# First stage of u and last step of a kernel block in 64-row tiles, in the slot behind PV

## The chip, the core and the metric

One core of a Trainium2 chip (trn2). The metric is the device time of one execution in microseconds; three timed runs of the kernel before are at hand, and one profiled execution. Engines: PE multiplies matrices, ACT, DVE and POOL do element-wise work, SP issues the DMAs. PSUM is the memory that PE writes; the kernel holds it as eight tiles of 128 rows by 512 columns.

## What is computed

Two independent parts, whose results stand side by side in the output. Part A is a long convolution of `u` with a kernel `K` that is first made from complex exponentials; part B is softmax attention with 16 heads of 28. L = S = 2048 and D = 448, all in float32.

```
K  = 2 * Re(einsum("dn,dnl->dl", C, exp(A*dt * pos)))       # 448 kernels of 2048
ya = irfft(rfft(u^T, 2L) * rfft(K, 2L))[:L]^T + u * D_skip
q, k, v = heads(x @ wqkv);  yb = softmax(q k^T * scale) v @ wo
out = concat([ya, yb], -1)
```

## The kernel before

Attention sets the frame. After a setup of some 250 us (projections, seeds of K, first maxima) a loop of 256 steps runs: 4 groups of 4 heads, 4 query chunks of 512, 16 key tiles of 128. Inside a step the order is written out by hand and kept on every engine:

```
ORDER = ('m0','s0','m1','s1','v','f','pv','f','v','k','m2','s2','m3','s3','v')
```

`m0` to `m3` are matmuls for row maxima of a later query chunk (tile `pm`, 128*128, emptied by ACT as `rl` for m0 and by DVE for the rest). `s0` to `s3` are score matmuls (tile `pss`), each followed by an exponential on ACT (`p`). `pv` adds up probabilities times values of the step before: four matmuls of 128 rows by 32 columns side by side into `po`. A matmul on plain float32 appears in the trace as two instructions, so pv counts as x8. The two `f` are slots: each takes at most one job of other work (`slot`). The first stands ahead of PV, the second behind it. `v` hands DVE one operation of a block's powers, `k` starts blocks and hands POOL theirs.

What the slots do, in the order of preference: urgent pieces of attention (sums, scale, end of maxima), output projections (`p_due`), pieces of kernel blocks (`m_due`), pieces of u (`u_due`), and, from step 192 on, the products of the spectra (`f_slot`).

- A *kernel block* `b` (56 of them, one begun every 3.5 steps) makes eight of the 448 kernels: two products of `e` and `g` (part0, `k_mm`), whose results ACT copies to `ko`, and a last step (part1): `ko` times the cosines and sines of `w1`, the first stage of its Fourier transform, copied by ACT to `yk` and stored. Their due steps are 4, 5 and 6 after the block's begin.
- *u*, the transform of the input, has a first stage of 16 jobs (`u_stage1`) and a second of 16 (`u_stage2`). A job of the first loads rows of u (tile `ua`), multiplies by the cosine half of `w1` in one slot and by the sine half in another, copies both by ACT to `ub`, and stores to `yu_d`. The second reads `yu_d` with the constants `m2u`.

`w1` is block diagonal: four blocks of 32 by 32 in 128 rows by 128 columns, one half for cosines and one for sines. `mm32` cuts a product into column tiles of 32. Of the four column tiles that a row of the array meets, three hold zeros for it.

The jobs and the maxima take their PSUM tiles from one ring of three (`w_tile`): `pm0`, `pm1`, `pm2` in turn. A matmul into a tile waits until the tile's last user has been emptied.

Of the kernel before, what the change touches and what calls it, by code (L numbers as in the profile page):

```python
# [18 lines left out]
D = 448  # L19
# [71 lines left out]
def body(ctx, tc, a, out):  # L91
# [25 lines left out]
    nc.sync.dma_start(ident, a["ident"])  # L117
    sel = const.tile([128, HG], F32, name="sel")
    kones = const.tile([128, 1], F32, name="kones")
    w1 = const.tile([128, 2, 128], F32, name="w1")  # L120

    att, k0_st = ExitStack(), ExitStack()
    ps_w, n_ring = [None, 3], [0]
# [12 lines left out]
    def mm32(o, w, x_, start, stop, at=0):  # L136

        for i in range(w.shape[-1] // 32):
            c = slice(32 * i, 32 * i + 32)
            nc.tensor.matmul(o[c], w[:, c], x_, start=start, stop=stop, tile_position=(0, at + 32 * i))  # L140


    kt_g, kd_g, q_u, m_u, mh_u, o_u, rl_u = {}, {}, {}, {}, {}, {}, {}

# [67 lines left out]
    with ExitStack() as st:  # L212
# [54 lines left out]
        half_pi = s_p.tile([128, 1], F32, name="half_pi")  # L267
        nc.gpsimd.memset(half_pi, TWO_PI / 4)
        nc.sync.dma_start(sel, a["sel"])
        nc.sync.dma_start(w1, a["w1"])  # L270
        for k in range(NCK):
            for s in (1, 0):
                src = wns[k][:, s, :].rearrange("p (g h e) -> p g h e", g=G, e=DH)
# [293 lines left out]
    def u_stage1(q):  # L567
        t_ = {}

        def load():  # L570
            u_in = t_["in"] = kq_p.tile([128, 8, CI], F32, name="ua", bufs=2)[:, :4]
            for j in range(4):
                nc.sync.dma_start(u_in[32 * j:32 * j + 32], bass.AP(
                    tensor=u_a.tensor, offset=u_a.offset + 4 * q * D + j * CI, ap=[[N2 * D, 32], [D, 4], [1, CI]]))

        def part(c):
            if c == 0:
                t_["out"] = kq_p.tile([128, 2, 4, CI], F32, name="ub", bufs=2)
            u_in, yt = t_["in"], t_["out"]
            pw = w_tile()  # L580
            mm32(pw[:, :D], w1[:, c, :], u_in.rearrange("p n i -> p (n i)"), start=True, stop=True)
            nc.scalar.activation(yt[:, c].rearrange("p n i -> p (n i)"), pw[:, :D], AF.Copy)
            if c == 1:
                for j in range(4):
                    nc.sync.dma_start(yu_d[8 * q:8 * q + 8, :, j * CI:(j + 1) * CI].rearrange("r k i -> k r i"),
                                      yt[32 * j:32 * j + 32].rearrange("p c n i -> p (c n) i"))
        return [load, lambda: part(0), lambda: part(1)]

    def u_stage2(m):
        t_ = {}  # L590
# [84 lines left out]
    def k_mm(b):  # L675
        t_ = {}

        def part0(i):
            pw = w_tile()
            e, g = egs[b] if i == 0 else egs.pop(b)  # L680
            for n, (h, c) in enumerate(((0, 0), (0, 1), (1, 0), (1, 1))):
                for j in range(4):
                    x_ = h * 8 + i * 4 + j
                    nc.tensor.matmul(pw[32 * j:32 * j + 32, :N2], g[:, c, x_, :], e[:, c, x_, :],
                                     start=n == 0, stop=n == 3, tile_position=(0, 32 * j))
            if i == 0:
                t_["ko"] = g_p.tile([128, 2, N2], F32, name="ko", bufs=2)
            nc.scalar.activation(t_["ko"][:, i], pw[:, :N2], AF.Copy)

        def part1():  # L690
            ko = t_["ko"]
            pw = w_tile()
            for i in range(2):
                for c in range(2):
                    mm32(pw[64 * c:64 * c + 64, i * 128:(i + 1) * 128], ko[:, i, :], w1[:, c, :], True, True, 64 * c)
            yk = g_p.tile([128, N1, 4, 2], F32, name="yk", bufs=2)
            nc.scalar.activation(yk.rearrange("p k j i -> p i j k"),
                                 pw[:, :256].rearrange("p (i j k) -> p i j k", i=2, j=4), AF.Copy)
            nc.sync.dma_start(yk_d[b // NBF][:, :, b % NBF], yk.rearrange("p (m k) j i -> p m (k j i)", k=4))
        return [lambda: part0(0), lambda: part0(1), part1]  # L700

# [178 lines left out]
            u_jobs[i][0]()  # L880

    def u_part(i, c):
        u_jobs[i][1 + c]()
        if c and i not in (14, 15):
            u_load(i + 2)
        if c and i == 15:
            u_load(16)
            u_load(17)
        if c and i == 31:
            load_wo()  # L890

    u_load(0)
    u_load(1)
    u_due = collections.deque((3 + UP * i + (UP / 2) * c + (4 if i > 15 else 0), i, c) for i in range(32) for c in range(2))
    k_due = collections.deque(range(NB))
    m_due = collections.deque()

# [56 lines left out]
        urgent.clear()  # L954
        urgent.extend(q)

    def slot(s_):
        n_slot[0] += 1
        if urgent and urgent[0][0] <= n_slot[0]:
            urgent.popleft()[2]()  # L960
        elif s_ >= NS and f_slot(s_, "s"):
            pass
        elif p_due and p_due[0][0] <= s_:
            p_due.popleft()[1]()
        elif m_due and m_due[0][0] <= s_:
            m_due.popleft()[1]()
        elif u_due and u_due[0][0] <= s_:
            u_part(*u_due.popleft()[1:])
        else:
            f_slot(s_, "s") or f_slot(s_, "f")  # L970
# [6 lines left out]
    def k_begin(s_):  # L977
        if not (k_due and K0 + k_due[0] * KP <= s_ and k_due[0] in egs and not powers["e"] and not powers["g"]):
            return
        b = k_due.popleft()  # L980
        k_start(b)
        powers["g"] += g_powers(b)
        powers["e"] += [lambda i=i, q=q: e_power(b, i, q) for i in range(3) for q in range(3)]
        p0, p1, p2 = k_mm(b)

        def m1():
            p1()
            done["mm"] = b
        m_due.extend((s_ + KD + i, t_) for i, t_ in enumerate((p0, m1, p2)))
        last[0] = b  # L990

    last = [None]
# [13 lines left out]
    for s in range(NS):  # L1006
        u, kt = divmod(s, NK)
        sm = s + NK + LEAD
        if s == 12 * NK:
            k0_st.close()  # L1010
            f_p["s", 0] = f_p["s", 1] = pool(f0_st, "f0_p", side="right")
            f_ready["s", 0], f_ready["s", 1] = s, NS
        if s >= 12 * NK and f_ready["s", 1] == NS and not (k_due or m_due or powers["g"] or powers["e"]):
            g_st.close()
            ps_st.close()
            ps_w[:] = pool(ps_st, "ps_f", 4, PSUM), 1
            f_ready["s", 1] = s + F1
        if kt == 12 and u // NQ == G - 1:
            load_og(u)
        late[0] = s + NK + LEAD > NS  # L1020
        if u % NQ == NQ - 1 and u < NU - 1 and kt % 4 == 2:
            load_v(u // NQ + 1, kt // 4)
        if sm < NS and sm // NK % NQ == NQ - 1 and sm % NK % 4 == 0 and sm % NK and sm // (NQ * NK) + 1 < G:
            load_kd(sm // (NQ * NK) + 1, sm % NK // 4 - 1)
        if sm < NS and sm % (NQ * NK) == 0 and sm:
            load_kd(sm // (NQ * NK), HG - 1)
        if kt % 4 == 1 and u % NQ == 1 and u // NQ + 1 < G:
            load_k(u // NQ + 1, kt // 4, k_pools[(u // NQ + 1) % 2])
        if kt == 2:
            if u + 2 < NU:  # L1030
                load_q(u + 2)
        ps = []
        for op in ORDER:
            if op[0] == "s":
                ps.append(s_mm(u, kt, int(op[1])))
            elif op[0] == "f":
                slot(s)
            elif op[0] == "v":
                vec()
            elif op == "k":  # L1040
                k_next()
                k_begin(s)
                k_seed(s)
                for _ in range(3):
                    if powers["e"]:
                        powers["e"].popleft()()
            elif op == "pv":
                if prev:
                    pv_step(*prev)
                    if prev[1] == NK - 1:  # L1050
                        fin(prev[0], s)
            elif sm < NS:
                max_mm(sm // NK, sm % NK, int(op[1]))
        for _ in range(FX if late[0] else 0):
            slot(s)
        if sm < NS and sm % NK == NK - 1:
            def end(un=sm // NK):
                max_end(un, w_tile())
                max_put(un)
            max_join(sm // NK)  # L1060
            soon_slot(UG[0], end)
        k_next()
        prev = (u, kt, ps)
# [11 lines left out]
def constants():  # L1075
# [9 lines left out]
    n1, k1 = np.arange(N1), np.arange(N1)  # L1085
    n2, k2 = np.arange(N2), np.arange(N2)
    th = 2 * np.pi * np.outer(n1, k1 + 0.25) / N1
    w1 = np.zeros((2, 128, 128))
    wb = np.zeros((2, 2, N1, 2, N1))
    for j in range(4):  # L1090
        w1[0, 32 * j:32 * j + 32, 32 * j:32 * j + 32] = np.cos(th)
        w1[1, 32 * j:32 * j + 32, 32 * j:32 * j + 32] = np.sin(th)
    for h in range(2):
        wb[h, 0, :, h, :] = np.cos(th).T / L
        wb[h, 1, :, h, :] = np.sin(th).T / L
    k["w1"] = w1.transpose(1, 0, 2)
    k["wb"] = wb.transpose(0, 1, 2, 4, 3).reshape(128, N2)
    ph = 2 * np.pi * ((k1[:, None, None] + 0.25) * n2[None, :, None] / L + n2[None, :, None] * k2[None, None, :] / N2)
    c, s = np.cos(ph).transpose(1, 0, 2), np.sin(ph).transpose(1, 0, 2)
    m2 = np.zeros((2, N2, N1, 2, 64))  # L1100
    m2[0, :, :, 0], m2[0, :, :, 1] = c, s
    m2[1, :, :, 0], m2[1, :, :, 1] = -s, c
    k["m2u"] = m2.reshape(2, 16, 4, N1, 128).transpose(1, 0, 2, 3, 4).reshape(128, N1, 128)
    wa = np.zeros((2, 64, N1, N2, 2))
    ct, st = c.transpose(2, 1, 0), s.transpose(2, 1, 0)
    wa[0, ..., 0], wa[0, ..., 1] = ct, -st
# [23 lines left out]
```

## Time and profile before

| | |
|---|---|
| timed runs | 1301.66, 1305.03, 1306.4 us; median 1305.03 |
| profiled execution | 1301.1 us from the first to the last instruction (its span; the page has no other time for it) |
| PE busy | 1228.2 us, 94% of the span |
| ACT, DVE, POOL busy | 952.4, 948.0, 871.1 us |
| u, first stage on PE | 256 instructions of 448 columns |
| last steps of blocks on PE | 896 instructions of 128 columns |
| ACT copies | `ub` 128x448 x32, mean 550 ns; `yk` 128x256 x56, mean 703 ns |

A row of the order of time reads: start, length, engine, line, operation, out<-in, rows*columns of the tile, shape, count; in brackets what the engine waited for. Matmuls run into each other, so a row's length holds the end of the pipe too, and the distance of starts tells what a matmul costs. `w` is `w1` (numbers are left out of names). All rows of the loop have line 75, the helper that records them; names tell them apart.

### The profile page before, as it was taken

The numbers are of one execution on the slowest core, as the hardware profiler recorded it, in microseconds if no ns is written. First come the engines' busy times: TensorE is split into PE (matmuls) and PEld (weight loads), VectorE is DVE, ScalarE is ACT, GpSimd is POOL, SyncE is SP. The second block draws the span as 40 slices with busy tenths as digits, with TensorE's granted clock in tenths as the row PEclk, the third lists the DMA queues.
The fourth block names the chain that finished last, engine by engine and source line by source line (L and its number), as shares of the span: only waits on it lengthen the run. The fifth ranks groups of instructions, "written<-read, shape, count | busy, mean of one in ns | idle before, by whom it ended". The sixth has DMA issues, their size and how long they took to land.

```text
span 1301.1 us, 33177 instructions
## 1 busy us (share of the span) xinstructions
PE 1228.2 (94%) x12625; PEld 701.0 (54%) x12625; DVE 948.0 (73%) x2106; ACT 952.4 (73%) x2068; POOL 871.1 (67%) x736
## 2 busy tenths in 40 slices
PE   6878985899999999999999999999999999999997
PEld 5657763355555555555555555555555555544433
DVE  5887896987777887787788888888888655645111
ACT  4775763488888888888888888888887766756552
POOL 3676683298888878888869999998996212424421
PEclk9888997999999999999999999999999999999999
DMA  6677769835866555458644131733425453647656
GB/s 194 203 258 244 249 206 294 237 77 124 195 137 149 124 146 148 140 147 231 181 126 96 54 95 32 182 91 83 103 51 148 153 158 133 201 144 244 198 162 174
DMA packets 200088, 205.35 MB, mean 158 GB/s; under 512 B 95993, under 2 KB 158521, under 8 KB 197881
## 3 DMA queue, kind: packets, MB, share of 16 engines
q1 hardware_dynamic: 199928, 203.23, 56.2%
q8 instruction: 100, 1.64, 0.5%
q14 instruction: 60, 0.48, 0.1%
HBM read 120.73 MB, written 82.18 MB: 156 GB/s over the span
## 4 chain that ended last, share of the span: by engine, by line
PE 71%; DVE 10%; DMA 6%; POOL 5%; ACT 3%; issue 3%; SPq 0%; POOLq 0%; ACTq 0%; DVEq 0%
PE pm L75 40%; PE pss L75 16%; PE po L75 15%; DVE tri L75 2%; DVE mx L75 2%; POOL e L75 1%; POOL qhat L75 1%; DMA k<-hl 1%; ACT tri L75 1%; DVE qhat L75 1%; DVE sg L75 1%; DMA tri<-in_B_wqkv 1%; DVE px L75 1%; DMA khat<-k 1%; DMA ut<-in_A_u 1%
## 5 line engine op out<-in xcount | busy, mean ns | idle before, releaser
L75 ACT ACTIVATE p<-pss 128x512 f32<-128x512 f32 x1024 | 560.9, 609 | 111.6 <-PE pss L75 108.6
L75 PE MATMUL pss<-qhat,khat 128*128 128x512 f32 x1024 | 402.5, 399 | 1.5 <-ACT p L75 1.4
L75 DVE TENSOR_REDUCE mx<-pm 128x1 f32<-128x512 f32 x500 | 321.4, 684 | 109.2 <-PE pm L75 107.1
L75 PE MATMUL pm<-khat,qhat 128*128 128x512 f32 x749 | 326.3, 438 | 3.4 <-DVE mx L75 2.1
L75 POOL TENSOR_TENSOR e<-e,sdb 128x256 f32<-128x256 f32 x168 | 202.0, 1202 | 116.2 <-ACT e L75 61.2
L75 PE MATMUL po<-p,v 128*32 128x512 f32 x2048 | 269.1, 594 | 0.0
L75 POOL TENSOR_TENSOR e<-e,eu 128x256 f32<-128x256 f32 x168 | 248.4, 1478 | 13.2
L75 PEld LDWEIGHTS pm<-khat,qhat 128*128 128x128 f32 x749 | 141.0, 189 | 199.7 <-ACT p L75 47.8
L75 DVE CUSTOM_DVE_ANT_0 rl<-pm,rl 128x512 f32<-128x512 f32 x249 | 171.4, 688 | 65.2 <-ACT rl L75 61.5
L75 PEld LDWEIGHTS pss<-qhat,khat 128*128 128x128 f32 x1024 | 190.2, 188 | 45.7 <-issue 10.8
L75 POOL TENSOR_TENSOR eu<-e,sdb 128x256 f32<-128x256 f32 x168 | 202.2, 1203 | 0.0
L75 POOL TENSOR_TENSOR p<-pr,pr 64x448 f32<-64x448 f32 x64 | 73.3, 1145 | 158.5 <-PE pm L75 133.2
L75 ACT ACTIVATE rl<-pm 128x512 f32<-128x512 f32 x249 | 150.8, 606 | 20.4 <-PE pm L75 20.4
L75 DVE TENSOR_TENSOR g<-g,zg 128x128 f32<-128x128 f32 x392 | 162.1, 413 | 3.4
L75 PE MATMUL pm<-xh,khat 112*128 112x512 f32 x256 | 94.1, 451 | 23.2 <-DVE hl L75 11.1
L75 PE MATMUL pm<-kdif,qhat 128*128 128x512 f32 x249 | 100.5, 404 | 2.6 <-DMA v<-v 1.3
L75 DVE TENSOR_TENSOR zg<-g,zg 128x128 f32<-128x128 f32 x224 | 88.0, 393 | 5.0
L75 PEld LDWEIGHTS pm<-e,g 128*32 128x32 f32 x3584 | 57.2, 109 | 43.8 <-issue 16.1
L75 DVE TENSOR_TENSOR pr<-pm,ub 128x448 f32<-128x448 f32 x64 | 37.0, 619 | 56.4 <-PE pm L75 42.0
L75 PEld LDWEIGHTS pm<-xh,khat 112*128 112x128 f32 x256 | 54.2, 217 | 39.4 <-DVE hl L75 12.9
L75 PE MATMUL pm<-e,g 128*32 128x64 f32 x3584 | 73.0, 222 | 1.9 <-POOL e L75 1.9
L75 ACT ACTIVATE y<-pm 128x448 f32<-128x448 f32 x48 | 26.5, 553 | 58.2 <-PE pm L75 33.8
(134 smaller groups left out, 1470.3 us busy)
## 6 DMA issues: line engine op xcount, KB each, us to landing
sdb<-sd SPq DMA_DIRECT2D x56, 336.0 KB
khat<-k SPq DMA_DIRECT2D x64, 256.0 KB
qhat<-q SPq DMA_DIRECT2D x64, 256.0 KB
sd<-sg SPq DMA_DIRECT2D x8, 1456.0 KB
k<-hl SPq DMA_DIRECT2D x16, 512.0 KB
q<-hl SPq DMA_DIRECT2D x16, 512.0 KB
mw<-in_mw SPq DMA_DIRECT2D x16, 512.0 KB
sd<-qhat SPq DMA_DIRECT2D x8, 896.0 KB
```

Of the source, the lines that this page charges most:

```text
L75: i = f(*args, **kw)
```

## The change

`w1` becomes `w2`, of the same size, without the zeros. Each product has a contraction of 64 rows instead of 128, and there are two of them for the two halves of the rows, at row positions 0 and 64, each into a PSUM tile of its own.

- First stage of u: one job (`both`) instead of two halves. It takes two tiles of the ring, issues eight matmuls of 64 rows by 32 columns and 448 columns of u, and two ACT copies of 128x448. Whole rows of u are loaded, in two DMAs instead of four; the store is one DMA instead of four. The order of rows in `yu_d` changes, and the constant `m2u` with it.
- Last step of a block: sixteen matmuls of 64 rows by 32 columns and 64 columns of `w2` instead of eight of 128 rows and 128 columns; two tiles of the ring; two ACT copies of 128x128 instead of one of 128x256.
- `slot` learns whether it stands behind PV. Ahead of PV the two-tile jobs (a block's last step, u's first stage) are passed over, and the next kind in the order of preference may go.

```diff
+        def both():
+            pw = [w_tile() for _ in range(2)]
+            for i in range(4):
+                c = slice(32 * i, 32 * i + 32)
+                for h in range(2):
+                    nc.tensor.matmul(pw[h][c, :D], w2[half[h], 0, c], t_["in"][half[h]], start=True, stop=True,
+                                     tile_position=(64 * h, 32 * i))
+            yt = kq_p.tile([128, 2, D], F32, name="ub", bufs=2)
+            for h in range(2):
+                nc.scalar.activation(yt[:, h], pw[h][:, :D], AF.Copy)
+            nc.sync.dma_start(yu_d.rearrange("(q h r) k d -> q (r k) h d", q=16, h=2)[q], yt)
...
         def part1():
             ko = t_["ko"]
-            pw = w_tile()
+            pw = [w_tile() for _ in range(2)]
             for i in range(2):
                 for c in range(2):
-                    mm32(pw[64 * c:64 * c + 64, i * 128:(i + 1) * 128], ko[:, i, :], w1[:, c, :], True, True, 64 * c)
+                    for j in range(2):
+                        for r in range(2):
+                            n = 64 * c + 32 * j
+                            nc.tensor.matmul(pw[r][n:n + 32, 64 * i:64 * i + 64], ko[half[r], i, 32 * j:32 * j + 32],
+                                             w2[half[r], 1, 64 * c:64 * c + 64], start=True, stop=True, tile_position=(64 * r, n))
...
-            nc.scalar.activation(yk.rearrange("p k j i -> p i j k"),
-                                 pw[:, :256].rearrange("p (i j k) -> p i j k", i=2, j=4), AF.Copy)
+            for r in range(2):
+                nc.scalar.activation(yk[:, :, 2 * r:2 * r + 2].rearrange("p k j i -> p i j k"),
+                                     pw[r][:, :128].rearrange("p (i j k) -> p i j k", i=2, j=2), AF.Copy)
...
-    u_due = collections.deque((3 + UP * i + (UP / 2) * c + (4 if i > 15 else 0), i, c) for i in range(32) for c in range(2))
+    u_due = collections.deque((3 + UP * i + (UP / 2) * c + (4 if i > 15 else 0), i, c) for i in range(32) for c in range(2) if i > 15 or c)
...
-    def slot(s_):
+    def slot(s_, second=True):
...
-        elif m_due and m_due[0][0] <= s_:
+        elif m_due and m_due[0][0] <= s_ and (second or not m_due[0][2]):
             m_due.popleft()[1]()
-        elif u_due and u_due[0][0] <= s_:
+        elif u_due and u_due[0][0] <= s_ and (second or u_due[0][1] > 15):
...
-                slot(s)
+                slot(s, "pv" in ORDER[:n])
```

More of the change, by code (lines that the diff above doesn't have):

```diff
@@ L119, in body @@
     kones = const.tile([128, 1], F32, name="kones")
-    w1 = const.tile([128, 2, 128], F32, name="w1")
+    w2 = const.tile([128, 2, 128], F32, name="w2")
     att, k0_st = ExitStack(), ExitStack()
@@ L140, in mm32 @@
             nc.tensor.matmul(o[c], w[:, c], x_, start=start, stop=stop, tile_position=(0, at + 32 * i))
+    half = [slice(0, 64), slice(64, 128)]
     kt_g, kd_g, q_u, m_u, mh_u, o_u, rl_u = {}, {}, {}, {}, {}, {}, {}
@@ L269, in body @@
         nc.sync.dma_start(sel, a["sel"])
-        nc.sync.dma_start(w1, a["w1"])
+        nc.sync.dma_start(w2, a["w2"])
         for k in range(NCK):
@@ L570, in load @@
         def load():
[L571 to L579, printed above, removed]
-            pw = w_tile()
[L581 to L587, printed above, removed]
+            u_in = t_["in"] = kq_p.tile([128, 8, CI], F32, name="ua", bufs=2).rearrange("p n i -> p (n i)")[:, :D]
+            for h in range(2):
+                nc.sync.dma_start(u_in[half[h]], u_a.rearrange("(p q h) d -> q h p d", q=16, h=2)[q, h])
+        def both():
[6 more added lines that the diff above has]
+            yt = kq_p.tile([128, 2, D], F32, name="ub", bufs=2)
+            for h in range(2):
+                nc.scalar.activation(yt[:, h], pw[h][:, :D], AF.Copy)
+            nc.sync.dma_start(yu_d.rearrange("(q h r) k d -> q (r k) h d", q=16, h=2)[q], yt)
+        return [load, both]
     def u_stage2(m):
@@ L691, in part1 @@
             ko = t_["ko"]
-            pw = w_tile()
+            pw = [w_tile() for _ in range(2)]
             for i in range(2):
                 for c in range(2):
-                    mm32(pw[64 * c:64 * c + 64, i * 128:(i + 1) * 128], ko[:, i, :], w1[:, c, :], True, True, 64 * c)
+                    for j in range(2):
[3 more added lines that the diff above has]
+                                             w2[half[r], 1, 64 * c:64 * c + 64], start=True, stop=True, tile_position=(64 * r, n))
             yk = g_p.tile([128, N1, 4, 2], F32, name="yk", bufs=2)
-            nc.scalar.activation(yk.rearrange("p k j i -> p i j k"),
-                                 pw[:, :256].rearrange("p (i j k) -> p i j k", i=2, j=4), AF.Copy)
+            for r in range(2):
+                nc.scalar.activation(yk[:, :, 2 * r:2 * r + 2].rearrange("p k j i -> p i j k"),
+                                     pw[r][:, :128].rearrange("p (i j k) -> p i j k", i=2, j=2), AF.Copy)
             nc.sync.dma_start(yk_d[b // NBF][:, :, b % NBF], yk.rearrange("p (m k) j i -> p m (k j i)", k=4))
@@ L882, in u_part @@
     def u_part(i, c):
-        u_jobs[i][1 + c]()
+        u_jobs[i][1 + c if i > 15 else 1]()
         if c and i not in (14, 15):
@@ L988, in m1 @@
             done["mm"] = b
-        m_due.extend((s_ + KD + i, t_) for i, t_ in enumerate((p0, m1, p2)))
+        m_due.extend((s_ + KD + i, t_, i == 2) for i, t_ in enumerate((p0, m1, p2)))
         last[0] = b
@@ L1032, in body @@
         ps = []
-        for op in ORDER:
+        for n, op in enumerate(ORDER):
             if op[0] == "s":
@@ L1087, in constants @@
     th = 2 * np.pi * np.outer(n1, k1 + 0.25) / N1
-    w1 = np.zeros((2, 128, 128))
+    w2 = np.zeros((2, 2, 64, 2, 64))
     wb = np.zeros((2, 2, N1, 2, N1))
-    for j in range(4):
-        w1[0, 32 * j:32 * j + 32, 32 * j:32 * j + 32] = np.cos(th)
-        w1[1, 32 * j:32 * j + 32, 32 * j:32 * j + 32] = np.sin(th)
+    for c, t in enumerate((np.cos(th), np.sin(th))):
+        for j in range(2):
+            w2[0, :, j::2, c, 32 * j:32 * j + 32] = t
+            w2[1, :, 32 * j:32 * j + 32, c, 32 * j:32 * j + 32] = t
     for h in range(2):
@@ L1095, in constants @@
         wb[h, 1, :, h, :] = np.sin(th).T / L
-    k["w1"] = w1.transpose(1, 0, 2)
+    k["w2"] = w2.reshape(2, 128, 128).transpose(1, 0, 2)
     k["wb"] = wb.transpose(0, 1, 2, 4, 3).reshape(128, N2)
@@ L1102, in constants @@
     m2[1, :, :, 0], m2[1, :, :, 1] = -s, c
-    k["m2u"] = m2.reshape(2, 16, 4, N1, 128).transpose(1, 0, 2, 3, 4).reshape(128, N1, 128)
+    k["m2u"] = m2.reshape(2, 2, 16, 2, N1, 128).transpose(2, 3, 0, 1, 4, 5).reshape(128, N1, 128)
     wa = np.zeros((2, 64, N1, N2, 2))
```

## The prediction

> **What bounds the kernel now.** I read the page first, then busy time by stretches, then the order of time on PE and ACT inside single steps.
>
> ```profile
> span 1301.1 us, 33177 instructions
> PE 1228.2 (94%) x12625; PEld 701.0 (54%) x12625; DVE 948.0 (73%) x2106; ACT 952.4 (73%) x2068; POOL 871.1 (67%) x736
> PE   6878985899999999999999999999999999999997
> PE 71%; DVE 10%; DMA 6%; POOL 5%; ACT 3%; issue 3%; SPq 0%; POOLq 0%; ACTq 0%; DVEq 0%
> 290.00:460.00 170.00, 169.42 (x2045) 92.85 (x2044) 132.84 (x316) 141.30 (x317) 138.31 (x108) 1.00 0.63 143
> 700.00:900.00 200.00, 199.35 (x2443) 114.22 (x2435) 174.71 (x418) 169.78 (x385) 188.70 (x150) 1.00 0.41 95
> ```
>
> The columns of the last two rows are PE, PEld, DVE, ACT, POOL, granted clock, DMA share and GB/s. In both stretches PE has no free time and the clock is whole, and most of the chain that ended last is PE. POOL, next in line, has 11.3 us of 200 left at 700 to 900. So in the stretches in which both changed steps run, what PE does or waits for in a step is what the step costs. A step starts anew with each PV group (po). Two pieces of PE in order of time, the first with a kernel block's last step (ko), the second with half a u job (ua,w):
>
> ```profile
> 718.30 1.04 PE L75 MATMUL po<-p,v 128*32 128x512 f32 x8
> ...
> 720.99 0.40 PE L75 MATMUL pss<-qhat,khat 128*128 128x512 f32 x1
> 721.32 0.64 PE L75 MATMUL pm<-w,ko 128*32 128x128 f32 x16
> 721.78 1.04 PE L75 MATMUL po<-p,v 128*32 128x512 f32 x8
> 722.75 0.50 PE L75 MATMUL pm<-khat,qhat 128*128 128x512 f32 x1
> 723.09 0.40 PE L75 MATMUL pss<-qhat,khat 128*128 128x512 f32 x1
> 723.33 0.39 PE L75 MATMUL pm<-khat,qhat 128*128 128x512 f32 x1
> 723.56 0.40 PE L75 MATMUL pss<-qhat,khat 128*128 128x512 f32 x1
> ...
> 724.82 1.06 PE L75 MATMUL po<-p,v 128*32 128x512 f32 x8
> ```
>
> ```profile
> 360.33 1.04 PE L75 MATMUL po<-p,v 128*32 128x512 f32 x8
> 361.19 0.94 PE L75 MATMUL pm<-ua,w 128*32 128x448 f32 x8
> 362.06 0.50 PE L75 MATMUL pm<-khat,qhat 128*128 128x512 f32 x1
> 362.40 0.40 PE L75 MATMUL pss<-qhat,khat 128*128 128x512 f32 x1
> 362.64 0.40 PE L75 MATMUL pm<-khat,qhat 128*128 128x512 f32 x1
> ...
> 364.12 0.64 PE L75 MATMUL po<-p,v 128*32 128x512 f32 x4
> ```
>
> A step with no job takes 724.82 - 721.78 = 3.04 us. The step with a block's last product (ko) takes 721.78 - 718.30 = 3.48, so that job is worth 0.44. The step with one half of a u job takes 364.12 - 360.33 = 3.79, so a half is worth 0.75 and both 1.50. Changing from one tile shape to another costs time too. Matmuls of one shape follow each other at 0.23 (723.33 to 723.56), but pss to ko takes 0.33: 0.10 to enter. PV to u, both 128*32, takes 0.86, PV to pm, 128*128, 0.97: 0.11 to leave. The first pm then takes 0.34 to its follower, 0.11 more than 0.23, because its weights were not loaded ahead.
>
> **The change on PE, per u job (16 of them).** Two halves become one job of eight tiles. If the two row halves run beside each other, as four column tiles do now, streaming stays that of one half, 0.75. Four more tiles must be issued, though. The first row here has the most instructions in the least time, the last one serves the next part:
>
> ```profile
> 318.58 0.44 PE L75 MATMUL pm<-sel,o 128*32 128x4 f32 x32
> 318.86 1.06 PE L75 MATMUL po<-p,v 128*32 128x512 f32 x8
> ...
> 717.83 0.65 PE L75 MATMUL pm<-e,g 128*32 128x64 f32 x32
> ```
>
> 32 instructions pass in 318.86 - 318.58 = 0.28, so 9 ns each, and four more tiles are 0.035. No row shows PE going from 128*32 to 64-row tiles. Bounds: nothing, if rows are switched like columns inside one shape, or 0.22, as much as leaving to 128*128 costs. I take 0.11, since the tiles stay 32 columns wide and entering them cost 0.10. That is 0.75 + 0.035 + 0.11 = 0.90 before waits.
>
> The Trainium skill, "TensorEngine Tiling (Array Packing)", section Key Properties, says that a change of tiling mode, not of tile, drains TensorE; it speaks against this change, and by it the 0.11 is paid 72 times. The trace shows that drain between 128*128 and 128*32 (0.10 and 0.11), and not between the two shapes at issue.
>
> **The same per kernel block (56).** Eight matmuls of 128 columns (16 instructions) become sixteen of 64 (32 instructions). Overlap halves the streaming, 0.44 to 0.22, but 32 instructions took 0.28 even with 4 columns each, and that is what I take. Without overlap it is that of the e,g row, 32 instructions of 64 columns in 718.30 - 717.83 = 0.47. With the shape change: 0.28 + 0.11 = 0.39 against 0.44. In the order of the two programs 49 of the 56 last steps stood ahead of PV and 7 behind it; now all are behind, next to PV, which was already of 32 columns, so before neither place paid a second change of shape.
>
> **The new wait.** Three PSUM tiles go round. After a job that takes two, the step's third pm matmul gets the tile of the second (or of a job ahead of PV), and its fourth, m3, gets the job's first tile. Before, m3 had the tile of the second or of a job ahead of PV, both long emptied. m3's weight load stands in PE's queue with pss and all that follows behind it, and it now waits until ACT has emptied the job's first tile. What ACT does after the u half above:
>
> ```profile
> 362.19 0.55 ACT L75 ACTIVATE ub<-pm 128x448 f32<-128x448 f32 x1 [0.40 <-PE pm L75]
> 362.63 0.30 ACT L75 ACTIVATE g<-sdb 128x128 f32<-128x128 f32 x1
> 362.90 1.09 ACT L75 ACTIVATE p<-pss 128x512 f32<-128x512 f32 x2
> ```
>
> A step of before in which a block's last step stood behind PV, first PE, then ACT:
>
> ```profile
> 821.54 1.04 PE L75 MATMUL po<-p,v 128*32 128x512 f32 x8
> 822.40 0.62 PE L75 MATMUL pm<-w,ko 128*32 128x128 f32 x16
> ...
> 823.52 0.39 PE L75 MATMUL pm<-khat,qhat 128*128 128x512 f32 x1
> ...
> 825.14 0.67 PE L75 MATMUL po<-p,v 128*32 128x512 f32 x4
> ```
>
> ```profile
> 823.09 0.69 ACT L75 ACTIVATE yk<-pm 128x256 f32<-128x256 f32 x1 [0.98 <-PE pm L75]
> 823.53 0.36 ACT L75 ACTIVATE g<-sdb 128x128 f32<-128x128 f32 x1
> 824.05 1.09 ACT L75 ACTIVATE p<-pss 128x512 f32<-128x512 f32 x2 [0.17 <-PE pm L75]
> ```
>
> For u the first copy would end at 362.19 + 0.55 = 362.74. A load that starts then gives a matmul that streams 0.11 later, at 362.85, where m3 now starts at 362.64: a wait of 0.21. For a block the copy is half of yk's:
>
> ```profile
> L75 ACT ACTIVATE yk<-pm 128x256 f32<-128x256 f32 x56 | 39.4, 703 | 3.9 <-PE pm L75 3.9
> L75 ACT ACTIVATE ko<-pm 128x64 f32<-128x64 f32 x112 | 29.1, 259 | 8.3 <-PE pm L75 8.3
> ```
>
> Between 64 columns at 0.26 and 256 at 0.70, 128 are 0.41. The copy ends at 823.09 + 0.41 = 823.50, m3 at 823.61 instead of 823.52: 0.09. Bounds: nothing with a copy as short as ko's (823.46), and 0.37 with one as long as yk's now (823.09 + 0.69 + 0.11 = 823.89). For u the bounds are nothing and 0.42, twice the estimate, if ACT comes late to it.
>
> **The sum.** u: before 1.50, after 0.90 + 0.21 = 1.11, gain 0.39 x 16 = 6.2 us. Blocks: before 0.44, after 0.39 + 0.09 = 0.48, loss 0.04 x 56 = 2.2 us. Together 4 us: a span of 1297.1 instead of 1301.1. The three runs' median, 1305.0, lies 3.9 above that span, so I forecast **1301 us**.
>
> **What I cost at nothing.** A u job issues three DMAs where it issued eight, with rows of 1792 bytes for pieces of 448. SP saves five issues of about 0.44 us a job:
>
> ```profile
> L75 SPq DMA_DIRECT2D ua<-in_A_u x49: 311/430/1585, 288.8 to 434.3; - x49
> L75 SPq DMA_DIRECT2D yu_d<-ub x64: 302/450/1663, 273.8 to 461.1; - x64
> ```
>
> Neither is waited for by PE: the u tiles are loaded two jobs ahead, and PE's 169.42 of 170 us leave no room for it. If that cover were gone, a late load would stop PE with all that is queued behind, but the loads get smaller. The second read of u, of all its first stage, comes three steps after the last store, over 9 us, as before. ACT gets 56 more copies, but not more elements; it is busy 141.30 of 170 us. The jobs that lost their place ahead of PV leave it to u's second stage and to f jobs. From step 199 of 256 on both programs have the same order on PE, so the end moves with what is gained before.
>
> **The rivals.** (1) *No change of shape is paid*, because 64-row tiles of 32 columns follow 128*32 as one column tile follows another. All 72 jobs then save 0.11, 7.9 us: 1293 us. For it: PV and ua,w at 0.86 pay nothing for a new tile. Against it: both changes that the trace shows were paid.
>
> (2) *The wait at m3 does not appear*, because ACT empties the first tile earlier than I place it. That gives 0.21 x 16 + 0.09 x 56 = 8.4 us: 1293 us. Against it: ub began only 0.13 after the pm that follows its job, and takes 0.55.
>
> (3) *The two row halves run one after the other.* A u job is 1.50 + 0.035 + 0.11 + 0.21 = 1.86, 0.36 worse; a block 0.47 + 0.11 + 0.09 = 0.67, 0.23 worse. 16 x 0.36 + 56 x 0.23 = 18.6 us slower: 1324 us. No row shows two row halves. The Trainium skill, "TensorE: Matmul & The Clock Gate", section Part 3, gives nine tiles in three rows and three columns 6.3 times the rate of one, which speaks against this rival; nothing in the trace of before can show it.
>
> (4) *ACT becomes the brake behind a block's last step*, and this one is slower. A strided copy of half the columns may take as long as yk's whole 0.69, and two of them stand ahead of the exponentials that m3's followers and the next PV need. In the step at 821.54 one yk and one g were enough to start the exponentials at 824.05. PV began exactly when they ended, 824.05 + 1.09 = 825.14. That step took 3.60, 0.12 more than 3.04 + 0.44. With the full 0.37 instead of 0.09 at m3, 56 blocks lose 15.7 us more: 4 - 15.7, so 11.7 us slower than before, 1317 us. It decides against the change from a copy of 0.48 us on (0.07 more in 56 blocks), and by more than 0.5% from 0.60. Against it: 128x128 for g takes 0.30 to 0.36. After the change 18 of 56 blocks and 7 of 16 u jobs are followed by a step with nothing ahead of PV, where PV has the least time to spare: at 364.12 the exponentials had ended 0.13 before.
>
> **How the numbers follow.** A measurement here tells 0.5% from no change, 6.5 us. Forecast 38%: the gain at u and the loss at the blocks nearly cancel. Rival 1: 20%, rival 2: 15%, rival 3: 10%, rival 4: 17%. So faster 0.35, within 0.38, slower 0.17 + 0.10 = 0.27. The forecast's own range is 1297 to 1308 (half of the 0.11 one way, 0.09 more per job the other). The range over the cases goes from 1289, rivals 1 and 2 half together, to 1318, which takes in rival 4 and leaves out rival 3 and the case in which 1 and 2 both hold in full (1285).
>
> **What would show it.** Right: a step with the u job behind PV and nothing ahead takes about 3.04 + 0.90 + 0.21 = 4.15 and stands 16 times instead of 32 halves; steps with ko behind PV take 3.5; the job's start lies about 0.97 behind PV, not 0.86; m3's load waits for ACT ub or yk. Wrong: a handoff of 0.86 (rival 1), m3 0.23 after pss (rival 2), ko's 32 instructions over 0.4 (rival 3), PV waiting for ACT p in the steps after ko (rival 4). The forecast fails also if PE waits for something that it does not wait for now, POOL above all, with 11.3 us left in 200.

## The result, and the profile after

| | before | after |
|---|---|---|
| median of 14 runs, us | 1304.22 (1300.44 to 1306.55) | 1308.16 (1304.07 to 1311.35) |
| ratio, 95% interval | | 1.0034 [1.0024, 1.0044] |
| profiled execution: timed, span | span 1301.1 | timed 1304.07, span 1302.1 |

The changed kernel is 4 us slower where 4 us faster was forecast: inside the range, and on the wrong side. The page of after, and busy time in the same two stretches:

```profile
span 1302.1 us, 34964 instructions
PE 1228.9 (94%) x13521; PEld 679.7 (52%) x13521; DVE 951.9 (73%) x2106; ACT 955.5 (73%) x2124; POOL 869.6 (67%) x736
PE 70%; DVE 11%; DMA 6%; ACT 5%; POOL 4%; issue 3%; SPq 0%; ACTq 0%; POOLq 0%; DVEq 0%
290.00:460.00 170.00, 168.57 (x2279) 84.80 (x2276) 135.07 (x316) 141.88 (x330) 138.27 (x109) 1.00 0.55 146
700.00:900.00 200.00, 198.92 (x2684) 109.81 (x2683) 172.98 (x413) 169.31 (x396) 186.17 (x147) 1.00 0.39 93
```

PE still has next to no free time in either stretch and the clock is still whole, so the method of the prediction (count what a step costs on PE) holds for after too. What changed is small in these sums: PE idles 1.43 us of 170 where it idled 0.58, and 1.08 of 200 where it was 0.65. Busy time does not show the loss, since a matmul whose weights come late is shown as busy for longer (0.50 instead of 0.40). The order of time does. A step of after with a block's last step (ko), PE and then ACT:

```profile
718.92 1.06 PE L75 MATMUL po<-p,v 128*32 128x512 f32 x8
719.92 0.45 PE L75 MATMUL pm<-w,ko 64*32 64x64 f32 x32
720.30 0.51 PE L75 MATMUL pm<-khat,qhat 128*128 128x512 f32 x1
720.64 0.40 PE L75 MATMUL pss<-qhat,khat 128*128 128x512 f32 x1
720.98 0.50 PE L75 MATMUL pm<-khat,qhat 128*128 128x512 f32 x1
721.31 0.40 PE L75 MATMUL pss<-qhat,khat 128*128 128x512 f32 x1
721.54 0.39 PE L75 MATMUL pm<-kdif,qhat 128*128 128x512 f32 x1
...
722.56 1.07 PE L75 MATMUL po<-p,v 128*32 128x512 f32 x8
```

```profile
720.48 0.69 ACT L75 ACTIVATE yk<-pm 128x128 f32<-128x128 f32 x2 [0.23 <-PE pm L75]
...
368.75 0.98 ACT L75 ACTIVATE ub<-pm 128x448 f32<-128x448 f32 x2 [1.53 <-PE pm L75]
...
369.92 1.09 ACT L75 ACTIVATE p<-pss 128x512 f32<-128x512 f32 x2
```

The step takes 722.56 - 718.92 = 3.64. PV to ko is 1.00, and ko to m2, at 720.30, is 0.38. From s2 at 720.64 on, where each start should follow the last by 0.23, m3 follows by 0.34 and s3 by 0.33: 0.11 and 0.10 lost. ACT began the copies at 720.48. The weight loads of m3, s3 and the next step's m0 (kdif):

```profile
720.98 0.19 PEld L75 LDWEIGHTS pm<-khat,qhat 128*128 128x128 f32 x1 [0.38 <-ACT yk L75]
721.08 0.19 PEld L75 LDWEIGHTS pss<-qhat,khat 128*128 128x128 f32 x1
721.31 0.19 PEld L75 LDWEIGHTS pm<-kdif,qhat 128*128 128x128 f32 x1
```

m3's load waits for the copy, and m3 starts with it. The load of s3, the next matmul, starts 0.10 after m3. Where nothing waits, a load starts with the matmul ahead of it, as that of m0 does (721.31, with s3). So a late load delays the next one too. A u step of after (its ACT rows are ub and p above):

```profile
366.70 1.04 PE L75 MATMUL po<-p,v 128*32 128x512 f32 x8
367.68 0.98 PE L75 MATMUL pm<-ua,w 64*32 64x448 f32 x16
368.59 0.50 PE L75 MATMUL pm<-khat,qhat 128*128 128x512 f32 x1
368.92 0.40 PE L75 MATMUL pss<-qhat,khat 128*128 128x512 f32 x1
369.35 0.50 PE L75 MATMUL pm<-khat,qhat 128*128 128x512 f32 x1
369.68 0.40 PE L75 MATMUL pss<-qhat,khat 128*128 128x512 f32 x1
...
370.60 0.47 PE L75 MATMUL pss<-qhat,khat 128*128 128x512 f32 x1
371.00 0.68 PE L75 MATMUL po<-p,v 128*32 128x512 f32 x4
```

Here m3 follows s2 by 0.43 and s3 follows m3 by 0.33, 0.30 lost, and PV starts at 371.00, when the exponentials end (369.92 + 1.09). What PE's weight loads waited for between 290 and 1014 us (total, times, longest), after and then before, names the two copies:

```profile
PEld pm L75 <- ACT yk L75: 20.3, 51, 0.7
PEld pm L75 <- ACT ub L75: 12.3, 21, 0.8
```

```profile
PEld pm L75 <- ACT yk L75: 3.5, 8, 0.8
```

These totals are longer than what PE lost, because a load that waits does so partly while the matmul ahead of it still streams: in the ko step above it is 0.38 of waiting for 0.11 of delay.

The next table is worked out from the order of time on PE: medians of the distances between starts, over all steps of a kind with nothing ahead of the next PV, in us. "Two tiles of 128 rows" is an experiment told below. An empty step is 3.03 in both kernels.

| | empty | ko, two tiles of 128 rows (15 steps) | ko, after (17) | u, after (6) |
|---|---|---|---|---|
| PV to job | | 0.88 | 1.00 | 0.97 |
| job to m2 | 0.97 from PV | 0.55 | 0.38 | 0.91 |
| m2 to s2 | 0.34 | 0.34 | 0.34 | 0.34 |
| s2 to m3 | 0.23 | 0.23 | 0.33 | 0.42 |
| m3 to s3 | 0.23 | 0.23 | 0.34 | 0.34 |
| last score matmul to next PV | 0.33 | 0.33 | 0.32 | 0.39 |
| whole step | 3.03 | 3.49 | 3.64 | 4.29 |

By such medians, with and without e,g ahead of PV, a block's last step cost 0.455 before and 0.61 after, and a u job 2 x 0.76 = 1.52 before and 1.27 after. Where e,g stands ahead of the next PV, that PV is not late, and the u job costs 1.50 before and 1.20 after. So 56 x 0.155 = 8.7 us are lost and 16 x 0.25 to 16 x 0.30, 4.0 to 4.8, gained: the loop gets 3.9 to 4.7 us longer. The first exponential of the loop, which marks the end of the setup, in before and then in after:

```profile
254.70 1.08 ACT L75 ACTIVATE p<-pss 128x512 f32<-128x512 f32 x2
```

```profile
250.95 1.08 ACT L75 ACTIVATE p<-pss 128x512 f32<-128x512 f32 x2
```

From there to the end it is 1046.4 us before and 1051.15 after: 4.75 longer, about what the steps say. The profiled execution of after had a setup 3.75 shorter and is itself 4 below its median, which is why the two spans differ by 1.0 only.

### The profile page after: what moved, and what is told of

Its sections match the earlier page's. It is cut to its first block, busy times and chain, and to the rows that moved or that the text cites. A ratio compares the mean times of both kernels' runs of the same rounds, so it can differ in the third digit from the quotient of the medians.

```text
span 1302.1 us, 34964 instructions
## 1 busy us (share of the span) xinstructions
PE 1228.9 (94%) x13521; PEld 679.7 (52%) x13521; DVE 951.9 (73%) x2106; ACT 955.5 (73%) x2124; POOL 869.6 (67%) x736
## 4 chain that ended last, share of the span: by engine, by line
PE 70%; DVE 11%; DMA 6%; ACT 5%; POOL 4%; issue 3%; SPq 0%; ACTq 0%; POOLq 0%; DVEq 0%
PE pm L75 39%; PE pss L75 15%; PE po L75 15%; DVE tri L75 2%; DVE mx L75 2%; ACT p L75 1%; POOL e L75 1%; DVE sg L75 1%; DMA sd<-qhat 1%; ACT tri L75 1%; ACT rl L75 1%; DVE px L75 1%; DVE qhat L75 1%; DVE rl L75 1%; DVE g L75 1%
## 5 line engine op out<-in xcount | busy, mean ns | idle before, releaser
L75 DVE TENSOR_REDUCE mx<-pm 128x1 f32<-128x512 f32 x500 | 325.8, 684 | 107.6 <-PE pm L75 104.6
L75 PE MATMUL pm<-khat,qhat 128*128 128x512 f32 x749 | 333.6, 448 | 6.2 <-DVE mx L75 2.2
L75 PE MATMUL pm<-xh,khat 112*128 112x512 f32 x256 | 90.7, 437 | 21.4 <-DVE hl L75 10.5
L75 PEld LDWEIGHTS po<-p,v 128*32 128x32 f32 x2048 | 51.8, 109 | 41.1 <-issue 36.1
```

Source lines behind the costliest of these rows:

```text
L75: i = f(*args, **kw)
```

## The experiments

Two theories stood at first. A: all that counts lies in the steps behind the two-tile jobs, the change of shape and the wait at m3. B: the placement costs, because jobs that were ahead of PV are pushed behind it and others are displaced. All ratios are to before.

### Each half of the change alone

u alone: the blocks' `part1` and its place as before, with `w1` loaded beside `w2` in the setup.

```diff
+    w1 = const.tile([128, 2, 128], F32, name="w1")
...
         nc.sync.dma_start(w2, a["w2"])
+        nc.sync.dma_start(w1, a["w1"])
...
-        m_due.extend((s_ + KD + i, t_, i == 2) ...
+        m_due.extend((s_ + KD + i, t_, False) ...
```

> Only u's first stage is changed (64-row tiles, two PSUM tiles, behind PV, whole rows); the blocks' last step is that of before. Theory A (account by step: 0.13 us for the change of shape, 0.30 at m3 for the copy of the first tile, streaming halved): a u job costs 1.27 instead of 1.50, so about 4 us less than before, ratio 0.997, and PV to the job 0.98, pss to m3 0.42. Theory B (the loss of the changed kernel comes from the place behind PV, where ACT is late for the next PV): u loses too, ratio 1.000 to 1.002.

Blocks alone: `u_stage1`, `u_due` and `m2u` as before, and the same second constant.

> Only the blocks' last step is changed; u's first stage is that of before. Theory A: a block costs 0.61 instead of 0.45, 56 times: about 9 us more than before, ratio 1.007. Theory B: also slower, by 4 us or more, but then one128 is slower by as much.

u alone 1305.92 us, 1.0019 [1.001, 1.0027]; blocks alone 1318.03, 1.0107 [1.0094, 1.012]. Both are slower than their loops can explain. In their profiles the loop begins at 259.4 and 261.0 us instead of 254.7. The suspect was the second constant, so the next pair loads it behind the setup, where the loop starts (`w1` for u alone, `w2` for blocks alone):

```diff
-        nc.sync.dma_start(w1, a["w1"])
...
+    nc.sync.dma_start(w1, a["w1"])
     prev = None
```

> u_only, with the constants of the blocks' last step (which u_only needs beside those of u) loaded at the loop's start and not in the setup. In u_only the loop was 3.7 us shorter than before, as theory A has it, and the setup 5.3 us longer. If the extra load in the setup makes that: 4 us less than before, ratio 0.997. If not: 1.002 as in u_only.

> k_only, with its second constant loaded at the loop's start. Loop of k_only: 6 us longer than before. If the extra load in the setup makes the rest: ratio 1.005 to 1.007; if not, 1.011 as in k_only.

u alone, constant late: 1301.33, 0.9979 [0.9971, 0.9987], 2.7 us faster. Blocks alone, constant late: 1312.17, 1.0057 [1.0044, 1.0071], 7.5 us slower. Together +4.8, and the whole change measured +4: the halves add up. The blocks lose 1.2 us less than their steps say (8.7), and u gains 1.3 to 2.1 less (4.0 to 4.8). To see the constant by itself, before with an unused second constant of the same 128 KB in the setup:

```diff
         nc.sync.dma_start(w1, a["w1"])
+        nc.sync.dma_start(w2, a["w2"])
```

> The kernel before, with one more constant of 128 KB loaded in the setup behind w1 and never used. If this is what u_only and k_only lost against u_late and k_late: 5 to 6 us more than before, all ahead of the loop, ratio 1.004 to 1.005. If not: 1.000.

1309.06, 1.0043 [1.0029, 1.0057]. That is 4.7 us. Most of it lies ahead of the loop, whose first exponential is:

```profile
259.12 0.59 ACT L75 ACTIVATE p<-pss 128x512 f32<-128x512 f32 x1
```

It comes 4.4 later than in before. In the eleven profiled executions without a second constant in the setup it starts between 250.95 and 256.25, in the three with one at 259.12, 259.43 and 260.98. Why an unread load takes that long stays open. So the 4.6 us (1305.92 - 1301.33) and 5.9 us (1318.03 - 1312.17) between the first pair and the second are that constant's, or mostly so, and not the change's.

### The placement alone, and two tiles alone

Before, with the blocks' last step allowed behind PV only (`slot` as in the change), one tile, one copy:

```diff
+        elif m_due and m_due[0][0] <= s_ and (second or not m_due[0][2]):
```

> The kernel before, with the blocks' last step only behind PV, otherwise untouched (one tile, one copy, 128 rows). Theory A: 0.44 to 0.46 a block as before, 0.1 more in the 18 steps that are followed by a step with nothing ahead of PV: 0 to 2 us more than before, ratio 1.000 to 1.002. Theory B: most of the blocks' loss is here: 5 us or more, ratio 1.004 or above.

The same with two tiles and two copies, matmuls still 128 rows high:

```diff
-            pw = w_tile()
+            pw = [w_tile() for _ in range(2)]
...
-                    mm32(pw[64 * c:64 * c + 64, i * 128:(i + 1) * 128], ko[:, i, :], w1[:, c, :], True, True, 64 * c)
+                    mm32(pw[i][64 * c:64 * c + 64, :128], ko[:, i, :], w1[:, c, :], True, True, 64 * c)
```

> The kernel before, with the blocks' last step in 128-row tiles as before, but in two PSUM tiles with two copies (one for each half of the columns), only behind PV. No 64-row shape, no halved streaming. Theory A: PV to the job stays 0.86, streaming 0.44, the wait at m3 is 0.20 as in the changed kernel: a block costs 0.66, about 11 us more than before, ratio 1.009. Theory B: as one128.

Placement alone: 1304.1, 1.0006 [0.9997, 1.0014]. It costs nothing that can be measured, and B falls. Two tiles of 128 rows: 1304.29, 1.0007 [0.9996, 1.0018], where a loss was expected from the wait at m3. PE in one of its steps:

```profile
710.91 1.06 PE L75 MATMUL po<-p,v 128*32 128x512 f32 x8
711.79 0.62 PE L75 MATMUL pm<-w,ko 128*32 128x128 f32 x16
712.34 0.50 PE L75 MATMUL pm<-khat,qhat 128*128 128x512 f32 x1
712.68 0.40 PE L75 MATMUL pss<-qhat,khat 128*128 128x512 f32 x1
712.92 0.40 PE L75 MATMUL pm<-khat,qhat 128*128 128x512 f32 x1
```

m3 follows s2 by 0.24: no wait, although the ring and the number of copies are those of the changed kernel and the first copy is hardly shorter (median 0.42, in after 0.44). The difference is when it starts. The copies of this step:

```profile
712.26 0.70 ACT L75 ACTIVATE yk<-pm 128x128 f32<-128x128 f32 x2
```

The first starts 0.08 ahead of m2 (712.34); in after it starts 0.18 behind m2 (720.48 against 720.30). By the medians two things make up these 0.26. The copy starts 0.10 earlier after the job's own start (0.47 instead of 0.57): here all matmuls of the first tile come before those of the second, while with two row halves both tiles are filled side by side. And m2 starts 0.17 later, since the job streams 0.55 instead of 0.38, which covers more of the copy. No run separates the two. This run also isolates the shape: PV to job is 0.88, in after 1.00 (0.882 and 0.996), at the same place and with the same ring.

### The order of m and s behind the job

The changed kernel, with score matmuls first in the step behind a two-tile job, so that m3 stands 0.23 later on PE (`two[0]` says that this step's job took two tiles):

```diff
+SWAP = {'m2': 's2', 's2': 'm2', 'm3': 's3', 's3': 'm3'}
...
         for n, op in enumerate(ORDER):
+            if two[0] and op in SWAP:
+                op = SWAP[op]
```

> The changed kernel, but in a step whose slot behind PV took a two-tile job, each score matmul goes ahead of its maxima matmul (s2, m2, s3, m3). m3 comes 0.23 later, and ACT has by then emptied the job's first tile. Theory A (the price is m3's wait): the wait of 0.22 a block goes nearly whole, that of u (0.30) by a third or more, since m0 of the next step then waits for the second tile: 12 to 14 us less than the changed kernel, ratio to before 0.993 to 0.995. Theory D (the wait only moves, to the next m0 or to PV behind late exponentials): ratio 1.000 or above.

1302.14, 0.9984 [0.9973, 0.9995]: some 6 us better than the changed kernel. A step with ko, then one with u, PE:

```profile
711.19 0.46 PE L76 MATMUL pm<-w,ko 64*32 64x64 f32 x32
711.57 0.50 PE L76 MATMUL pss<-qhat,khat 128*128 128x512 f32 x1
711.91 0.40 PE L76 MATMUL pm<-khat,qhat 128*128 128x512 f32 x1
712.14 0.40 PE L76 MATMUL pss<-qhat,khat 128*128 128x512 f32 x1
712.38 0.39 PE L76 MATMUL pm<-khat,qhat 128*128 128x512 f32 x1
...
356.44 0.50 PE L76 MATMUL pss<-qhat,khat 128*128 128x512 f32 x1
356.78 0.39 PE L76 MATMUL pm<-khat,qhat 128*128 128x512 f32 x1
357.01 0.40 PE L76 MATMUL pss<-qhat,khat 128*128 128x512 f32 x1
357.24 0.46 PE L76 MATMUL pm<-khat,qhat 128*128 128x512 f32 x1
357.63 0.50 PE L76 MATMUL pm<-kdif,qhat 128*128 128x512 f32 x1
```

Behind ko, m3 (712.38) no longer waits, and the median step falls from 3.64 to 3.56: s1 of the next step follows m1 by 0.33, so a late weight load there takes 0.10 of the gain back. 56 x 0.08 is 4.5 us; the rest of the 6 is not accounted for. Behind u nothing is gained: m3 to the next m0 is now 0.39, and the median step stays 4.30 (4.29 in after). The wait has moved, since a ring of three with two tiles just taken leaves one, and the matmuls that need the other two only changed places.

Two more attempts to hide it for u, both on top of u alone with the late constant. The first swaps m and s in the next step's first two pairs as well:

> u_late, with the score matmul ahead of the maxima matmul behind a u job and in the first two pairs of the next step. Theory A: no wait for the ring, a u job costs 0.75 + 0.035 + 0.13 = 0.92 to 0.98 instead of 1.50 in the kernel before: 8 to 9 us less than before, ratio 0.993 to 0.994. Theory D: as u_late, 0.997, or above.

1306.89, 1.0016 [1.0004, 1.0028], worse than u alone. Now a score matmul waits for ACT, which is late with the exponentials:

```profile
361.76 0.50 PE L76 MATMUL pss<-qhat,khat 128*128 128x512 f32 x1 [0.25 <-ACT p L76]
```

The second lets DVE copy the second tile and keeps the first swap:

```diff
-            for h in range(2):
-                nc.scalar.activation(yt[:, h], pw[h][:, :D], AF.Copy)
+            nc.scalar.activation(yt[:, 0], pw[0][:, :D], AF.Copy)
+            nc.vector.tensor_copy(yt[:, 1], pw[1][:, :D])
```

> u_late, with DVE and not ACT copying a u job's second tile, and s2, m2, s3, m3 in the step behind a u job. In swap the wait of a u job only moved from m3 to the next m0, and in u_swap2 to the next score matmul, which waits for ACT's exponentials. Theory E (the brake behind a u job is ACT with two copies of 0.44 each ahead of the exponentials): with one copy gone from ACT the wait goes, a u job costs 0.95 to 1.0 instead of 1.50: 8 to 9 us less than before, ratio 0.993 to 0.994. Rival (DVE's copy waits behind its other work or holds up m2's maxima): as u_late, 0.998, or above.

1300.66, 0.9972 [0.9961, 0.9983], not to be told from u alone. The wait stands at the next m1 (0.48 behind s0 by the median, where 0.23 is no wait), whose tile DVE empties late because it copied first. The same for both parts of the change:

> The changed kernel (u and blocks) with DVE copying the second tile of both, and s2, m2, s3, m3 behind both. Theory E: u as in u_dve_swap, a block 0.13 + 0.28 = 0.41 to 0.43 instead of 0.45: 9 to 11 us less than before, ratio 0.992 to 0.993. Rival: DVE, busy 174.7 of 200 us between 700 and 900, becomes the brake of the blocks: ratio 0.997 or above.

1305.51, 1.0007 [0.9995, 1.0019]. The median block step is 3.65, as without any of it.

### The copy's length

The changed kernel, with the blocks' two copies written in the order in which they lie in PSUM. K then has its values in another order; the instructions, their order and the number of elements stay.

```diff
-                nc.scalar.activation(yk[:, :, 2 * r:2 * r + 2].rearrange("p k j i -> p i j k"),
-                                     pw[r][:, :128].rearrange("p (i j k) -> p i j k", i=2, j=2), AF.Copy)
+                nc.scalar.activation(yk.rearrange("p k j i -> p (k j i)")[:, 128 * r:128 * r + 128], pw[r][:, :128], AF.Copy)
```

> The changed kernel, but ACT writes a block's two copies in the order in which they lie in PSUM, without the turn to yk's order; so the kernel K reaches the spectra in the wrong order. Nothing else differs. Theory A (what a block pays is m3's wait for the first copy, and the strided copy of 0.44 us is a part of it): a plain copy of 128 columns takes about 0.30, so m3's wait falls from 0.22 to about 0.08: 56 x 0.14 = 8 us less than the changed kernel, ratio to before 0.997 to 0.998. Rival (the wait does not hang on the copy's length): ratio 1.003 as the changed kernel.

1299.59, 0.9962 [0.9947, 0.9976]: some 9 us less than the changed kernel. The copies (minimum, median, maximum in ns), in after and then here:

```profile
L75 ACT ACTIVATE yk<-pm x112: 378/456/546, 272.8 to 1017.3; 128x128 f32<-128x128 f32 x112
```

```profile
L75 ACT ACTIVATE yk<-pm x112: 257/277/346, 276.1 to 1012.6; 128x128 f32<-128x128 f32 x112
```

And one of its steps on PE:

```profile
707.10 1.06 PE L75 MATMUL po<-p,v 128*32 128x512 f32 x8
708.10 0.45 PE L75 MATMUL pm<-w,ko 64*32 64x64 f32 x32
708.48 0.50 PE L75 MATMUL pm<-khat,qhat 128*128 128x512 f32 x1
708.81 0.40 PE L75 MATMUL pss<-qhat,khat 128*128 128x512 f32 x1
709.05 0.44 PE L75 MATMUL pm<-khat,qhat 128*128 128x512 f32 x1
709.33 0.39 PE L75 MATMUL pss<-qhat,khat 128*128 128x512 f32 x1
```

The copy is 0.18 shorter by the median, m3 follows s2 by 0.24 and s3 follows m3 by 0.28, and the median step is 3.48 instead of 3.64. 56 x 0.16 = 9.0 us, what was measured. PV to ko is still 1.00. So the length of the turned copy, through the wait at m3, accounts for all that made the blocks lose. What remains, 3.48 - 3.03 = 0.45, is what the last step cost before: the job to m2 is 0.17 shorter than with 128 rows (0.38 against 0.55), and the shape change (0.11) and the 0.05 still lost at s3 eat that.

## Why the prediction was wrong, step by step

**What held.** The bound (PE, step by step). The two row halves overlap: 32 instructions of 64 columns from ko to m2 take 0.38 with 0.11 for leaving, so 0.27, where 0.28 was taken; rival 3 is out. The Trainium skill, "TensorE: Matmul & The Clock Gate", Part 3, where tiles in different rows and columns run at the same time, agrees. The shape change between two tilings is paid: PV to job 0.996 against 0.882 for blocks and 0.972 against 0.858 for u, 0.114 for both, where 0.11 was assumed; rival 1 is out. This agrees with the drain at a change of mode in "TensorEngine Tiling (Array Packing)", Key Properties, of the Trainium skill. Before the wait, then, a block is 0.996 + 0.384 - 0.972 = 0.41 by the medians (0.39 forecast) and a u job 0.972 + 0.912 - 0.972 = 0.91 (0.90 forecast). The placement of the blocks costs nothing that can be measured, as taken; the DMAs, also taken at nothing, no run isolates. That the wait at m3 appears was right too, which leaves rival 2 out.

**What failed: the size of the wait at m3.** For blocks 0.09 was forecast, and 0.10 + 0.11 = 0.21 is lost by the medians; for u 0.21 was forecast, and 0.19 + 0.11 = 0.30 is lost, and with nothing ahead of it PV starts another 0.06 late. So the signs that the prediction named, 3.5 for a step with ko and 4.15 for one with u, came out as 3.64 and 4.29. In the ko step shown, the prediction's own sum goes wrong in three places. It took the start of the copy from the step of before at 821.54, whose m2 is

```profile
822.95 0.50 PE L75 MATMUL pm<-khat,qhat 128*128 128x512 f32 x1
```

- The first copy starts 0.18 after m2 (720.48 - 720.30), and was taken at 0.14 (823.09 - 822.95), from that step, in which one tile was copied.
- It lasts 0.44 (the median of the first copies; 0.456 is that of both), where 0.41 was interpolated between copies of 64 and 256 columns.
- The matmul starts 0.05 after the first copy's end by the median, but with its weights not loaded ahead its follower comes another 0.11 late, as m2's does (0.34 instead of 0.23). The prediction put 0.11 in all for this, where it is 0.16.

0.04 + 0.03 + 0.05 is 0.12, and 0.09 + 0.12 = 0.21. For u the copy's length was right (0.55, measured 0.54); its start, 0.16 after m2 instead of 0.13, and the same late load make 0.08 of the 0.09. On 56 blocks 0.12 is 6.7 us; on the u steps 0.09 on 16 jobs and 0.06 on some 7 are 1.9 us; the two turn -4 into about +4.6. Nothing else moved that much: the jobs before the wait cost 0.02 and 0.01 more than forecast, some 1.2 us against the change, and what the steps cost before was taken at 0.44 and 1.50 and is 0.455 and 1.52, 1.2 us in its favour. That the length of the copy sets the wait is shown by the run with the plain copy, and that a copy that starts earlier against m2 leaves no wait by the run with two tiles of 128 rows; that a late load costs some 0.10 of its own is read from the order of time and of the loads alone.

**Rival 4** had the place and the cause of the slowdown (the turned copy) but not the size: its copy as long as 0.69 is 0.456, below the 0.48 from which it was to decide. The sign turned at a shorter copy because the copy begins later and the late weight load costs more than the sum had it. Its second half, PV waiting for exponentials, is absent behind blocks (0.32 from the last score matmul to PV, in an empty step 0.33) and small behind u (0.39).

**What stays open.** Neither a ring of four tiles nor filling the first row half's tile ahead of the second's was tried. Three versions that keep K's order are faster than both kernels: the change to u alone with the constant loaded late, 0.9979, the same with DVE's copy, 0.9972, and the whole change with m and s exchanged, 0.9984. Their intervals overlap. The plain copy, 0.9962, shows what a K stored in the order of PSUM would be worth; the readers of that order would have to be changed as well.

## What to carry to other kernels

When a job takes one more tile of a small ring, find the matmul that meets the tile again, and work out when the job's first tile is complete and how long the copy then has until that matmul. Two tiles filled one after the other, in a job that streams 0.55, hid the copy; two filled side by side, in 0.38, exposed it: the faster job had less time to cover its copy. A weight load that comes late costs the wait and then, here, some 0.10 more, because the next load is late too. The blocks were to gain 0.05 each ahead of the wait (0.39 against 0.44), and three small errors in one wait added up to 0.12: where the terms of a sum nearly cancel, its sign is hardly known.

## What the hardware showed that was not expected

- Loading an unused constant of 128 KB in the setup costs 4.7 us, most of it ahead of the loop.
- An ACT copy of 128 columns from PSUM takes 0.277 us in order and 0.456 turned (medians of 112).
- 32 instructions of 64 columns pass in 0.27 us on eight tiles in two row halves, where the e,g row of the prediction, also 32 instructions of 64 columns but on four column tiles, took 0.47.
- A weight load that had to wait costs about 0.10 us beyond the wait: the matmul starts 0.05 after the copy that frees its tile, and its follower comes 0.34 later instead of 0.23.
